# A convolution, a router and eight experts on one core: where the first hidden block lies, and when token rows are gathered

## The chip, the cores and the metric

The kernel runs on one core of a Trainium2 chip. The metric is device time in microseconds (us), the median of timed runs; the profile is of one execution of its own.

## The reference

```python
# first part: a causal convolution along the sequence, softmax weights per head
x_pad = concat([zeros((B, 6, D)), x], axis=1)          # B=8, S=3584, D=192
out = einsum('hk,bskhg->bshg', softmax(weight), windows(x_pad, 7))
# second part, on N = 28672 rows of it
do_compute = x @ w_skip > 0                            # about half of the rows
logits = xc @ w_gate                                   # 8 experts, the best one
gate_w = softmax(logits)[best]
h = maximum(xc @ w1[e], 0)                             # 192 -> 1024
y = gate_w * (h @ w2[e])                               # 1024 -> 192
out[do_compute] = xc + y
```

Rows that the skip score drops keep the convolution's value.

## The kernel before

**Phase 1** goes through the eight batches. For each, TensorE does the convolution, transposes the rows, makes the logits and, by products with one-hot tiles, a list for each expert of the rows that it has to work on. SyncE stores the convolved rows to the output tensor in DRAM (`store_y`, L338). The rows of four batches are in SBUF at a time, in pools that are closed one by one; the pool of batch 5 (`xlast`) becomes `wk3`, and its stores run while batch 7 is routed.

**Phase 2** works in 61 blocks of up to 256 rows of one expert (`us` is 1 or 2 groups of 128). Eight blocks (0 to 7, `NTAIL`) come from a list of the first five batches for experts 0 and 1 and run while the last batches are still routed; six more (8 to 13, one or two groups each) finish these experts from the final lists; the rest are six blocks of each other expert and 11 whose expert is read at run time. For one block:

- `gather` (L737): GpSimd reads the rows into `y` by an indirect DMA, one for each group of 128. There are seven `y` buffers.
- `prep` (L756 to L772): VectorE takes the largest magnitude (`yam`) and a power of two as scale (`ysc`), ScalarE and VectorE split the row into two f16 parts (`yt`), and SyncE transposes them by DMA into `m`. A block of two groups also needs half of a row of `m` copied to the upper partitions by ScalarE (L750).
- `up` (L807, L816): the **first product**, in banks of PSUM `ph`; ScalarE's relu writes the high part `hh` (L820), VectorE the rest `hl` (L822).
- `down` (L850 to L852): the **second product** into `po`, 48 matmuls for two groups. VectorE adds the scaled result to `y` (L832), GpSimd scatters `o` to the output rows (L834).

The program is in the order in which the code is written. In step n of the main loop come `up` of block n+1, with parts of `prep` of later blocks between its banks; the gathers of blocks up to n+5 (`AHEAD`); then `down` of block n, again with parts of `prep`. Before a gather in the first eight steps GpSimd copies one element of `hl` of block n+1 (`after`, `tick`, L732), so that the gather can't start before that part of the first product has been rounded. The table `PSEQ` says how many parts of `prep` of blocks 0 to 2 follow each of the eight heads of the last batch's convolution. The raw weights of an expert are loaded into the buffer `raw` (L206), of which there is one; `wt` holds them split in two f16 parts. Those of expert 2 are loaded from step 6 on. The weights of the first two experts are written back to a scratch tensor (L264).

Of the kernel before, what the change touches and what calls it, by code (L numbers as in the profile page):

```python
# [7 lines left out]
F32 = mybir.dt.float32  # L8
F16 = mybir.dt.float16
# [7 lines left out]
P = 128  # L17
B, S, D = 8, 3584, 192
H, KT = 8, 7
G = D // H  # L20
E, F = 8, 1024
NTOK = B * S
NF = F // P
# [13 lines left out]
BLK = 256  # L37
# [29 lines left out]
E1 = 3  # L67
PIECES = (2,)*5 + (6, 8, 8)

PSEQ = (0,0,0,3,4,4,4,4)  # L70

IL = 4
ROUND = 12582912.0
# [17 lines left out]
def conv_router_moe(ctx: ExitStack, tc: tile.TileContext, x, band, taps, router_weights, weights, out):  # L91
    nc = tc.nc
    const = ctx.enter_context(tc.tile_pool(name="const", bufs=1))
    wst = ctx.enter_context(tc.tile_pool(name="wst", bufs=1))
# [590 lines left out]
    def step7(h):  # L685

        if FIRST[h]:
            if h:
                after(xs[B - 1][0:1, 0, h * G:h * G + 1])
            gather(blocks[int(FIRST[h])])  # L690
        for _ in range(PSEQ[h]):
            prep_piece()
# [3 lines left out]
    def prep_piece():  # L696
        if not preps:
            if begun[0] == PREP0:
                return
            preps.append(prep(blocks[begun[0]]))  # L700
            begun[0] += 1
        if next(preps[0], preps) is preps:
            preps.pop(0)
            prep_piece()
# [26 lines left out]
    def after(t):  # L731
        nc.gpsimd.tensor_copy(tick, t)  # L732

    def gather(k, fixed=True):
        k.y = ybuf[k.n % DEPTH]
        for u in range(k.us):
            rows_apart(nc.gpsimd.indirect_dma_start(  # L737
                out=k.y[:, u, :], out_offset=None, in_=out[0:k.rows, :],
                in_offset=bass.IndirectOffsetOnAxis(ap=k.si[:, u:u + 1], axis=0),
                bounds_check=k.rows - 1, oob_is_err=False), fixed)  # L740

    def paired(k):
        return k.us == 2 and NTAIL <= k.n < NBLK
# [39 lines left out]
    def bank(pools):  # L783
        pools.append(pools.pop(0))
        return pools[-1]

    def up(k, wt):
        k.hh = wk3.tile([P, NF, BLK], F16, tag="hh", bufs=2, name=f"hh{k.n}")
        k.hl = wk3.tile([P, NF, BLK], F16, tag="hl", bufs=2, name=f"hl{k.n}")
        w = k.us * P  # L790
        fs = 2 * BLK // w
        seq = ((OW1, 0), (OW1, 2), (OW1 + F, 1), (OW1L, 0), (OW1L + F, 1))
        phs = {}

        def open_bank(f0):
            phs[f0] = bank(ph_pools).tile([P, 2 * BLK], F32, tag="ph", name=f"ph{k.n}_{f0}").rearrange(
                "p (f w) -> p f w", w=w)

        if paired(k):

            for f0 in range(0, NF, fs):
                open_bank(f0)
            for a in range(0, NF, 2 * fs):
                for j in range(fs):
                    for f, p0, m in ((a + j, 0, 1), (a + fs + j, 64, 3)):
                        o = OW1L + F + f * P
                        nc.tensor.matmul(phs[f - j][:, j, :], wt[p0:p0 + 64, o:o + P], k.m[p0:p0 + 64, m, 0:w],  # L807
                                         start=(j == 0), stop=False, tile_position=(p0, 0), skip_group_check=True)
            seq = seq[:-1]
        for f0 in range(0, NF, fs):  # L810
            if not paired(k):
                open_bank(f0)
            ph = phs[f0]
            for f in range(f0, f0 + fs):
                for n, (o, m) in enumerate(seq):
                    nc.tensor.matmul(ph[:, f - f0, :], wt[:, o + f * P:o + (f + 1) * P], k.m[:, m, 0:w],  # L816
                                     start=(n == 0 and not paired(k)), stop=(n == len(seq) - 1),
                                     skip_group_check=paired(k))
            hh = k.hh[:, f0:f0 + fs, 0:w]
            nc.scalar.activation(hh, ph, AF.Relu)  # L820
            yield
            nc.vector.scalar_tensor_tensor(out=k.hl[:, f0:f0 + fs, 0:w], in0=ph, scalar=0.0, in1=hh,  # L822
                                           op0=ALU.max, op1=ALU.subtract)
# [36 lines left out]
    blocks = []  # L860
# [15 lines left out]
    NTAIL = len(blocks)  # L876
# [6 lines left out]
    NBLK = len(blocks)  # L883
# [40 lines left out]
    wk3 = ctx.enter_context(tc.tile_pool(name="wk3", bufs=2))  # L924
# [147 lines left out]
    gathered, prepped = AHEAD - 1, PREP0  # L1072
# [4 lines left out]
    for n in range(NBLK):  # L1077
        k = blocks[n]
        if listed and len(ph_pools) == 1:
            ph1.close()  # L1080
            wk4 = ctx.enter_context(tc.tile_pool(name="wk4", bufs=1))
            ps_h2 = ctx.enter_context(tc.tile_pool(name="ps_h2", bufs=2, space=PSUM))
            ph_pools.extend((ps_h2, ps_h, ps_h2, ps_h))
            ps_o2 = ctx.enter_context(tc.tile_pool(name="ps_o2", bufs=2, space=PSUM))
            po_pools.extend((ps_o2, ps_o2))
        nxt = 2 if n == NTAIL - 2 else k.e + 1 if k.e is not None and k.e >= NA and n == first_of[k.e] else E
        if nxt < E:
            wts[nxt] = new_wt(nxt)
            bg.append(split_weights(nxt, wts[nxt]))
        if n + 1 < NBLK and n + 1 == first_of.get(blocks[n + 1].e) and (blocks[n + 1].e or 0) >= NA:  # L1090
            background(-1)
        m = n + PREP + 1
        if m < NBLK and blocks[m].l is not None:
            l = blocks[m].l
            dynw[l] = wk4.tile([P, WW], F16, tag="wd", bufs=5, name=f"wd{l}")
            bg.append(dyn_weights(l, dynw[l]))
        far = n + 2
        while far < min(n + PREP + 1 + (n > 4), NBLK) and sum(q.us for q in blocks[n + 2:far]) < 4:
            far += 1
        while prepped < min(far, gathered):  # L1100
            ahead.append(prep(blocks[prepped]))
            prepped += 1
        if n + 1 < NBLK:
            upper_half(n + 1)
            weave(up(blocks[n + 1], weights_of(n + 1)), ahead, PU)
            upper_half(n + 2)
        ready = NBLK if listed and n > 3 else NTAIL
        if n + 1 >= NTAIL - 2:
            while prepped < min(n + 3, gathered):
                ahead.append(prep(blocks[prepped]))  # L1110
                prepped += 1
        while gathered < min(n + AHEAD + 1, ready):
            if n < NTAIL:
                after(blocks[n + 1].hl[0:1, 2 * (gathered % 3):2 * (gathered % 3) + 1, 0])
            gather(blocks[gathered])
            gathered += 1
        if n >= NTAIL - 2:
            next(saves, None)
        weave(down(k, weights_of(n)), ahead, PD)
        if n + 2 < NBLK and not hasattr(blocks[n + 2], "m"):  # L1120
            if prepped < n + 3:
                ahead.append(prep(blocks[prepped]))
                prepped += 1
            finish(ahead.pop(0))
        if n >= NTAIL + 8 and n % 2 == 0 and (n - NTAIL - 8) // 2 < NDYN:
            dyn_lists((n - NTAIL - 8) // 2)
# [4 lines left out]
    with tc.If(left > 0):  # L1131
# [10 lines left out]
        for e in range(E):  # L1142
            first = nc.values_load(lo_hi[0:1, e:e + 1], min_val=0, max_val=NTOK // BLK)
            last = nc.values_load(lo_hi[0:1, E + e:E + e + 1], min_val=0, max_val=NTOK // BLK)
            with tc.For_i(first, last, 1) as i:
                k = Blk()
# [69 lines left out]
```

## Time and profile before

| | us |
|---|---|
| runs | 655.3, 655.6, 663.0 |
| median | 655.6 |
| the profiled execution | 664.3 |
| its span on the core | 662.5 |
| TensorE busy in it | 624.5 |

The profile is of one execution, 8.7 us longer than the median of the runs. Its span leaves out 1.8 us of that execution. A busy time is the union of an engine's instructions, so TensorE was without a matmul for 38 us of the span. In its rows the bracket at the end is the time that the engine stood idle before the instruction and what ended it; "issue" is idle time that nothing in the records ends. PEclk is the granted clock as a share of full speed.

### The profile page before, as it was taken

To read this page: it belongs to the slowest core of one execution; us is meant where nothing else is said; L and a number is where in the kernel's file an instruction comes from. 1 tells how busy PE (TensorE), PEld (TensorE's weight loads), DVE (VectorE), ACT (ScalarE), POOL (GpSimd) and SP (SyncE) were. 2 spreads that over 40 slices of the span, in tenths; PEclk is the share of its full clock that TensorE was granted. 3 is DMA by queue.
4 is the path that set the end of the run, shared out by engine and by line. 5 is a ranking of instruction groups with operands and counts; after the bars stand their busy time and mean duration, and the time that the engine had idled before them with its cause. 6 is when DMAs were issued, how large, how long until landed. Compare 5 with 4: busy or idle time off the path is not lost.

```text
span 662.5 us, 18033 instructions
## 1 busy us (share of the span) xinstructions
PE 624.5 (94%) x6905; PEld 525.8 (79%) x6905; DVE 489.6 (74%) x1380; ACT 340.1 (51%) x665; POOL 266.5 (40%) x298
## 2 busy tenths in 40 slices
PE   7999999988899889999999998999999999999995
PEld 6555565556789778888989887899999988888995
DVE  4296989987797686787887885887878866666642
ACT  3687977876232254445545544544645544444421
POOL 4011111140444445445545545545545554444332
PEclk9999999998999899999999999999999999999998
DMA  8979797673562575773763662663673638999990
GB/s 339 427 328 372 300 400 315 238 236 126 177 197 67 151 186 151 222 196 79 181 188 80 174 187 63 181 178 79 169 191 86 185 79 255 238 337 234 281 241 13
DMA packets 93104, 134.64 MB, mean 203 GB/s; under 512 B 58268, under 2 KB 72670, under 8 KB 90576
## 3 DMA queue, kind: packets, MB, share of 16 engines
q1 hardware_dynamic: 81968, 111.37, 52.9%
q0 software_dynamic: 11040, 22.02, 12.8%
q8 instruction: 56, 0.92, 0.6%
q14 instruction: 40, 0.33, 0.2%
HBM read 72.10 MB, written 50.77 MB: 185 GB/s over the span
## 4 chain that ended last, share of the span: by engine, by line
PE 60%; DVE 1%; issue 1%; ACT 1%; another core or an unknown queue 0%; POOL 0%; POOLq 0%; ACTq 0%
PE ph L816 27%; PE po L852 10%; PE po L850 10%; PE po L851 10%; PE ph L807 4%; ACT hh L820 0%; DVE hl L822 0%; DVE am L214 0%; ACT yt L764 0%; ACT wt L235 0%; ACT m L750 0%; DVE yam L756 0%; DVE o L832 0%; POOL out_dram L834 0%
## 5 line engine op out<-in xcount | busy, mean ns | idle before, releaser
L820 ACT ACTIVATE hh<-ph 128x512 f16<-128x512 f32 x230 | 133.9, 593 | 235.5 <-PE ph L816 159.1
L822 DVE SCALAR_TENSOR_TENSOR hl<-ph,hh 128x512 f16<-128x512 f32 x230 | 157.2, 687 | 100.9 <-ACT hh L820 54.9
L850 PE MATMUL po<-wt,hh 128*128 128x192 f16 x768 | 189.6, 247 | 3.1 <-issue 3.0
L852 PE MATMUL po<-wt,hl 128*128 128x192 f16 x768 | 189.5, 247 | 2.9 <-issue 2.8
L851 PE MATMUL po<-wt,hh 128*128 128x192 f16 x768 | 189.5, 247 | 2.3 <-issue 2.1
L816 PE MATMUL ph<-m,wt 128*128 128x256 f16 (+1 forms) x1680 | 186.9, 269 | 1.7 <-DVE yam L759 1.0
L816 PEld LDWEIGHTS <-wt 128*128 128x128 f16 x1680 | 154.0, 98 | 27.5 <-issue 11.1
L834 POOL DMA_INDIRECT out_dram<-o,rows x82 | 86.4, 1054 | 143.2 <-DVE o L832 113.4
L737 POOL DMA_INDIRECT y<-out_dram,rows x82 | 85.6, 1044 | 25.2 <-issue 22.7
L850 PEld LDWEIGHTS <-hh 128*128 128x128 f16 x920 | 90.2, 98 | 6.0 <-issue 5.2
L852 PEld LDWEIGHTS <-hl 128*128 128x128 f16 x920 | 90.3, 98 | 5.5 <-issue 5.4
L851 PEld LDWEIGHTS <-hh 128*128 128x128 f16 x920 | 90.2, 98 | 4.6 <-issue 4.0
L769 DVE SCALAR_TENSOR_TENSOR yt<-y,ysc,yt 128x64 f16<-128x64 f32 x230 | 58.0, 312 | 3.6 <-ACT yt L764 3.4
L764 ACT ACTIVATE yt<-y,ysc 128x192 f16<-128x192 f32 x115 | 46.2, 447 | 27.7 <-DVE ysc L759 16.3
L832 DVE SCALAR_TENSOR_TENSOR o<-po,yf,y 128x192 f32<-128x192 f32 x115 | 46.4, 414 | 15.3 <-PE po L852 8.9
L313 ACT COPY xy<-pc 128x768 f32<-128x768 f32 x56 | 42.4, 813 | 8.7 <-PE pc L303 6.6
L235 ACT ACTIVATE wt<-raw,ar 128x512 f16<-128x512 f32 x56 | 40.5, 724 | 7.0 <-DVE ar L280 6.7
L303 PE MATMUL pc<-xy,toep 64*64 64x384 f32 x448 | 43.6, 499 | 0.5 <-ACT xy L313 0.5
L254 DVE SCALAR_TENSOR_TENSOR wt<-raw,ar,wt 128x512 f16<-128x512 f32 x56 | 41.7, 745 | 2.7 <-ACT wt L235 2.7
L357 POOL COPY yc<-xy 128x1024 f32<-128x1024 f32 x12 | 12.9, 1074 | 75.4 <-ACT xy L313 31.4
L376 PE MATMUL tp<-ident,xy 128*128 128x128 f32 x256 | 36.4, 285 | 6.9 <-ACT ya L313 4.7
L376 PEld LDWEIGHTS tp<-ident,xy 128*128 128x128 f32 x256 | 27.6, 142 | 18.5 <-ACT ya L313 6.4
(186 smaller groups left out, 814.8 us busy)
## 6 DMA issues: line engine op xcount, KB each, us to landing
xy<-in_x_dram SPq DMA_DIRECT2D x7, 3104.0 KB
wd<-wscr SPq DMA_DIRECT2D x44, 449.0 KB
wscr<-wt SPq DMA_DIRECT2D x84, 128.0 KB
raw<-in_weights_dram SPq DMA_DIRECT2D x16, 512.0 KB
out_dram<-xy SPq DMA_DIRECT2D x5, 1552.0 KB
out_dram<-xy SPq DMA_DIRECT2D x5, 1455.0 KB
raw<-in_weights_dram SPq DMA_DIRECT2D x16, 384.0 KB
out_dram<-xy SPq DMA_DIRECT2D x14, 388.0 KB
```

The lines of the kernel that those rows point to most:

```text
L376: nc.tensor.transpose(tp[:, u, :], src, ident)
L737: rows_apart(nc.gpsimd.indirect_dma_start(out=k.y[:, u, :], out_offset=None, in_=out[0:k.rows, :], in_offset=bass.IndirectOffsetOnAxis(ap= ...
L764: nc.scalar.activation(yt[:, u, 0:D], k.y[:, u, 0:D], AF.Copy, scale=sc[:, u:u + 1])
L769: nc.vector.scalar_tensor_tensor(out=yt[:, u, o:o + b_ - a], in0=k.y[:, u, a:b_], scalar=sc[:, u:u + 1], in1=yt[:, u, a:b_], op0=ALU.mult, ...
L816: nc.tensor.matmul(ph[:, f - f0, :], wt[:, o + f * P:o + (f + 1) * P], k.m[:, m, 0:w], start=(n == 0 and not paired(k)), stop=(n == len(se ...
L820: nc.scalar.activation(hh, ph, AF.Relu)
L822: nc.vector.scalar_tensor_tensor(out=k.hl[:, f0:f0 + fs, 0:w], in0=ph, scalar=0.0, in1=hh, op0=ALU.max, op1=ALU.subtract)
L832: nc.vector.scalar_tensor_tensor(out=o[:, u, 0:D], in0=po, scalar=f2[:, u:u + 1], in1=k.y[:, u, 0:D], op0=ALU.mult, op1=ALU.add)
L834: rows_apart(nc.gpsimd.indirect_dma_start(out=out[0:k.rows, :], out_offset=bass.IndirectOffsetOnAxis(ap=k.si[:, u:u + 1], axis=0), in_=o[: ...
L850: nc.tensor.matmul(pos[u], hh, w2(OW2, f), start=(f == 0), stop=False)
L851: nc.tensor.matmul(pos[u], hh, w2(OW2L, f), start=False, stop=False)
L852: nc.tensor.matmul(pos[u], hl, w2(OW2, f), start=False, stop=(f == NF - 1))
```

## The change

`up` takes the two halves of the relu's result of block 0 from the buffer of the raw weights, which nothing uses at that time, in place of two tiles of `wk3`. `PSEQ` does the parts of `prep` of blocks 0 to 2 earlier in the last batch. The step that gathers now copies an element of `hl` of the next block ahead of each block's gathers to the end, and in steps 4 and 5 it stops at two groups, from step 6 on at four.

```diff
-PSEQ = (0,0,0,3,4,4,4,4)
+PSEQ = (0,0,0,3,6,6,3,3)
...
     def up(k, wt):
-        k.hh = wk3.tile([P, NF, BLK], F16, tag="hh", bufs=2, name=f"hh{k.n}")
-        k.hl = wk3.tile([P, NF, BLK], F16, tag="hl", bufs=2, name=f"hl{k.n}")
+        if k.n == 0:
+            both = wst.tile([P, 2 * F + NF * D], F32, tag="raw", name="h0").bitcast(F16)[:, 0:2 * NF * BLK]
+            k.hh, k.hl = (both[:, o:o + NF * BLK].rearrange("p (f w) -> p f w", w=BLK) for o in (0, NF * BLK))
+        else:
+            k.hh = wk3.tile([P, NF, BLK], F16, tag="hh", bufs=2, name=f"hh{k.n}")
+            k.hl = wk3.tile([P, NF, BLK], F16, tag="hl", bufs=2, name=f"hl{k.n}")
...
+        room = 2 if n < NTAIL - 2 else 4
         while gathered < min(n + AHEAD + 1, ready):
-            if n < NTAIL:
-                after(blocks[n + 1].hl[0:1, 2 * (gathered % 3):2 * (gathered % 3) + 1, 0])
+            if ready == NBLK and blocks[gathered].us > room:
+                break
+            room -= blocks[gathered].us
+            f = 2 * (gathered % 3) if n < NTAIL else 2
+            after(blocks[n + 1].hl[0:1, f:f + 1, 0])
             gather(blocks[gathered])
             gathered += 1
```

TensorE's instructions keep their order; those of the other engines move at these places.

On ScalarE, at the first relu (`ph0_0` is the first bank of block 0; `lg6` and `lt6` are logits of batch 6, `ya7` rows of batch 7 on their way to a transpose). Before:

```order
L389 COPY lt6_1_2252<-pl6_1_2239 128x256 [waits PE_49,Activation_49]
L396 COPY lg6_1972<-pb6_1_2268 128x4x18 [waits PE_49]
L396 COPY lg6_1972<-pb6_1_2268 128x4x18
L764 ACTIVATE yt2_2282<-y2_233,ysc2_2263 128x192 [waits DMASW4_49,DVE_49]
L764 ACTIVATE yt2_2282<-y2_233,ysc2_2263 128x192 [waits DMASW5_49]
L820 ACTIVATE hh0_2311<-ph0_0_2313 128x512 [waits DMAHW5_49,DMAHW3_49,DMAHW6_49,DMAHW0_49,DMAHW7_49,PE_49,Activation_49]
L313 COPY ya7_0_2328<-tp7_0_0_2329 128x512 [waits PE_49]
```

And with the change:

```order
L389 COPY lt6_1_2260<-pl6_1_2247 128x256 [waits PE_49,Activation_49]
L764 ACTIVATE yt2_2267<-y2_233,ysc2_2230 128x192 [waits DMASW4_49,DVE_49]
L764 ACTIVATE yt2_2267<-y2_233,ysc2_2230 128x192 [waits DMASW5_49]
L396 COPY lg6_1972<-pb6_1_2278 128x4x18 [waits PE_49]
L396 COPY lg6_1972<-pb6_1_2278 128x4x18
L824 ACTIVATE h0_2311<-ph0_0_2312 128x512 [waits PE_49,Activation_49]
L313 COPY ya7_0_2327<-tp7_0_0_2328 128x512 [waits PE_49]
```

The relu no longer waits for the DMA queues (the stores of batch 5, whose place `wk3` takes); they are now waited for by the first relu of block 1. The split of block 2 has moved ahead of the logits of batch 6.

On GpSimd, at the end of the first eight blocks (`y1` is block 8's buffer, `y2` block 9's, `y3` block 10's, `y4` block 11's; L834 is the scatter). Before:

```order
L737 DMA y1_230<-out_0_dram,rows_224 128x194
L732 CAST tick_225<-hl5_3226 1x1
L737 DMA y2_233<-out_0_dram,rows_224 128x194 x2
L834 DMA out_0_dram<-o1_2299,rowsa_223 19840x194 x2
L732 CAST tick_225<-hl6_3406 1x1
L737 DMA y3_236<-out_0_dram,rows_224 128x194 x2
L834 DMA out_0_dram<-o2_2301,rowsa_223 19840x194 x2
L732 CAST tick_225<-hl7_3572 1x1
L737 DMA y4_239<-out_0_dram,rows_224 128x194
```

And with the change:

```order
L737 DMA y1_230<-out_0_dram,rows_224 128x194
L838 DMA out_0_dram<-o1_2299,rowsa_223 19840x194 x2
L732 CAST tick_225<-hl6_3398 1x1
L737 DMA y2_233<-out_0_dram,rows_224 128x194 x2
L838 DMA out_0_dram<-o2_2301,rowsa_223 19840x194 x2
L732 CAST tick_225<-hl7_3549 1x1
L737 DMA y3_236<-out_0_dram,rows_224 128x194 x2
L732 CAST tick_225<-hl7_3549 1x1
L737 DMA y4_239<-out_0_dram,rows_224 128x194
```

The gathers of blocks 9 and 10 are each a step later, and from step 8 on each block's gathers stand behind a copy of the next block's `hl`; there are 48 more of these copies in all.

On SyncE's queue, at the same place (`m9` and `m10` are the transposes of blocks 9 and 10, `raw2` loads of the raw weights of expert 2). Before:

```order
L772 DMA_TRANSPOSE m8_3457<-yt8_3441 128x3x128
L772 DMA_TRANSPOSE m9_3525<-yt9_3522 128x3x128 x2
L206 DMA raw2_3595<-in_weights_dram 128x1024 x2
L206 DMA raw2_3595<-in_weights_dram 128x768
L264 DMA wscr_63<-wt0_248 128x1024 x2
L206 DMA raw2_3595<-in_weights_dram 128x768
L772 DMA_TRANSPOSE m10_3671<-yt10_3631 128x3x128 x2
```

And with the change:

```order
L772 DMA_TRANSPOSE m8_3449<-yt8_3433 128x3x128
L206 DMA raw2_3572<-in_weights_dram 128x1024 x2
L206 DMA raw2_3572<-in_weights_dram 128x768
L264 DMA wscr_63<-wt0_248 128x1024 x2
L206 DMA raw2_3572<-in_weights_dram 128x768
L772 DMA_TRANSPOSE m9_3655<-yt9_3608 128x3x128 x2
L264 DMA wscr_63<-wt0_248 128x1024 x2
L772 DMA_TRANSPOSE m10_3802<-yt10_3759 128x3x128 x2
```

Block 9's transposes are now behind the loads of expert 2's raw weights, and block 10's behind two more stores. VectorE and ScalarE do the `prep` of blocks 9 and 10 a step later in the same way, ScalarE that of block 10 just ahead of the copy of block 9's upper half.

## Rows read from the trace of the kernel before

**Rows 1.** Page, part 1: busy us (share of span) x instructions.
```profile
PE 624.5 (94%) x6905; PEld 525.8 (79%) x6905; DVE 489.6 (74%) x1380; ACT 340.1 (51%) x665; POOL 266.5 (40%) x298
```

**Rows 2.** Page, part 4: the chain that ended last, by engine.
```profile
PE 60%; DVE 1%; issue 1%; ACT 1%; another core or an unknown queue 0%; POOL 0%; POOLq 0%; ACTq 0%
```

**Rows 3.** Timeline of PE, first relu: start, us, instruction [idle before <-releaser].
```profile
148.43 1.26 PE L816 MATMUL ph<-m,wt 128*128 128x256 f16 x10
152.39 1.60 PE L376 MATMUL tp<-ident,xy 128*128 128x128 f32 x8 [2.71 <-ACT ya L313]
154.04 2.33 PE L816 MATMUL ph<-m,wt 128*128 128x256 f16 x10
...
158.75 1.04 PE L376 MATMUL tp<-ident,xy 128*128 128x128 f32 x8
```

**Rows 4.** Timeline of ACT, the same place.
```profile
143.43 0.80 ACT L764 ACTIVATE yt<-y,ysc 128x192 f16<-128x192 f32 x2 [1.25 <-DVE ysc L759]
...
151.27 0.60 ACT L820 ACTIVATE hh<-ph 128x512 f16<-128x512 f32 x1 [3.82 <-DMA out_dram<-xy]
```

**Rows 5.** Windows: length, busy us (x) by engine, PEclk, DMA share, GB/s.
```profile
152.40:156.60 4.20, 4.20 (x24) 3.34 (x25) 2.83 (x8) 3.36 (x7) 0.00 (x0) 0.59 0.17 47
```

**Rows 6.** Timeline of DVE, the rest of batch 7's routing.
```profile
151.90 0.69 DVE L822 SCALAR_TENSOR_TENSOR hl<-ph,hh 128x512 f16<-128x512 f32 x1 [1.08 <-ACT hh L820]
...
157.04 0.69 DVE L822 SCALAR_TENSOR_TENSOR hl<-ph,hh 128x512 f16<-128x512 f32 x1 [1.57 <-ACT hh L820]
...
172.76 0.69 DVE L822 SCALAR_TENSOR_TENSOR hl<-ph,hh 128x512 f16<-128x512 f32 x1 [3.58 <-issue]
```

**Rows 7.** Timeline of PE, second product of block 5.
```profile
215.53 0.24 PE L852 MATMUL po<-wt,hl 128*128 128x192 f16 x1 [0.48 <-issue]
216.97 0.24 PE L850 MATMUL po<-wt,hh 128*128 128x192 f16 x1 [1.19 <-issue]
...
218.38 0.32 PE L852 MATMUL po<-wt,hl 128*128 128x192 f16 x1 [1.09 <-issue]
```

**Rows 8.** Timeline of POOL ahead of it and beside it.
```profile
208.27 1.06 POOL L737 DMA_INDIRECT y<-out_dram,rows  x1 [0.96 <-issue]
209.32 0.18 POOL L732 CAST tick<-hl 1x1 f32<-1x1 f16 x1
...
214.96 1.06 POOL L737 DMA_INDIRECT y<-out_dram,rows  x1 [0.16 <-issue]
216.32 1.01 POOL L737 DMA_INDIRECT y<-out_dram,rows  x1 [0.30 <-issue]
```

**Rows 9.** Windows, that second product (columns as in Rows 5).
```profile
213.50:222.26 8.76, 5.92 (x50) 5.13 (x48) 4.59 (x20) 1.96 (x5) 3.25 (x4) 0.81 0.22 58
```

**Rows 10.** Waits of PE: us in total, times, longest us.
```profile
PE po L850 <- issue: 4.0, 7, 1.2
PE po L852 <- issue: 3.3, 5, 1.1
PE po L851 <- issue: 2.3, 6, 0.9
...
PE ph L807 <- ACT m L750: 0.5, 2, 0.3
```

**Rows 11.** Windows, gathers (L737) alone, second products: length, POOL busy (x), PEclk, DMA.
```profile
252.58:258.39 5.81, 2.08 (x2) 1.00 0.65 198
391.89:396.26 4.37, 2.07 (x2) 1.00 0.33 88
...
419.57:424.57 5.00, 2.05 (x2) 1.00 0.79 220
...
501.80:505.86 4.06, 2.09 (x2) 1.00 0.46 108
```

**Rows 12.** Timeline of POOL and of DVE in one clean step.
```profile
333.01 1.05 POOL L737 DMA_INDIRECT y<-out_dram,rows  x1 [0.30 <-issue]
...
333.90 0.69 DVE L822 SCALAR_TENSOR_TENSOR hl<-ph,hh 128x512 f16<-128x512 f32 x1 [0.48 <-issue]
```

## The prediction

> **What bounds the kernel now.** I read the page's busy times first: TensorE is busy for 624.5 of 662.5 us [rows 1], and the chain that ended last is mostly its own [rows 2]. Its instructions keep their order, so the change is worth what it takes from or adds to TensorE's idle and slowed time. I then listed TensorE's waits by what ended them, and read the timelines at the two largest gaps and the windows around them. The reader is to see three things there.
>
> First, at 149.7 to 152.4 TensorE stands still for 2.71 us because ScalarE hasn't copied a PSUM tile [rows 3]. ScalarE stood 3.82 us in front of the first relu, until a store of rows had landed [rows 4]; the copy is the next in its queue. Right after the gap TensorE's granted clock is at its lower level for most of 152.4 to 156.6: 0.59 on average [rows 5], and ten matmuls take 2.33 us where they had taken 1.26 before [rows 3].
>
> Second, in the second product of block 5 TensorE creeps: idle times of 0.48, 1.19 and 1.09 us that end by "issue" [rows 7], while GpSimd has gathers in hand [rows 8]. The clock falls again, to 0.81 on average over 8.76 us [rows 9].
>
> Third, such "issue" waits come back all through phase 2, nearly all in second products: 4.0 + 3.3 + 2.3 = 9.6 us in all [rows 10]. No record says what holds the engine.
>
> **The two executions.** The sum is made against the profiled execution, 664.3 us (span 662.5 and 1.8 around it). The median of the runs is 8.7 us lower. The program is the same, so something that varies is missing in a typical run; the only candidate of that size in the trace is the "issue" waits (9.6) with the clock loss that follows the worst of them (8.76 x 0.19 = 1.7 [rows 9]). I take it that a typical run has (9.6 + 1.7 - 8.7) / 11.3, about a quarter, of them. The wait for the store isn't of this kind: it has its place in the order, and I count it whole in every run.
>
> **The change, part by part.**
>
> *The first relu in `raw`'s place.* The wait for the stores goes: the first relu then needs only its product. TensorE gains the 2.71 us of its gap, and, with no gap, the slow clock: 4.20 x (1 - 0.59) = 1.7 us [rows 5]; together 4.4. The bounds: at least what VectorE can follow. It does the rounding and batch 7's routing in between, and its idle times there that hang on the relu are 1.08 and 1.57 us, 2.65 in all [rows 6]; if VectorE were the bound from there on, no more than that would be gained. At most 4.4 + 1.25, if the wait of ScalarE for block 1's scale [rows 4] came out as well. I take 4.4, since VectorE has another 3.58 us of idle time before 172.8 [rows 6] in which it catches up. The wait itself moves to block 1's relu, the next user of `wk3`, which is four relus on in ScalarE's queue, with the copies of batch 7 between them: nothing. The buffer `raw` is next written for expert 2, after block 0 is done.
>
> *The scales a step earlier.* The scale of block 1 now comes before two list operations on VectorE, so the 1.25 us [rows 4] shrink; block 2's reduction may meet a gather that hasn't landed. Between 0 and 1.25 gained, already the upper bound above; I take 0, as ScalarE is not what TensorE waits for once the store is out of the way.
>
> *At most two groups in steps 4 and 5.* Before, the gathers of blocks 8, 9 and 10 were five, from 208.27 to 217.33, with two scatters between them [rows 8]; now there are one and two in these steps. If the crowd is what held TensorE, its gap (0.48 + 1.19 + 1.09 = 2.8) and the slow clock (1.7) go: 4.4 us of the profiled execution. If it isn't, 0. For a typical run I take a quarter to a third, 1.3.
>
> *Blocks 9 and 10 a step later.* Block 9's transposes now queue on SyncE behind the loads of `raw2`, and on ScalarE the copy of its upper half (L750) stands behind the split of block 10, which in turn needs a later gather. TensorE's nearest waits are those for such a copy elsewhere, 0.5 us for two [rows 10]. The trace has no larger one, so the upper bound is my choice: one short second product (24 of 48 matmuls, some 2 us) for each of the two blocks, 4. I take 0.5.
>
> *48 more copies on GpSimd.* Each takes 0.18 us [rows 8], and GpSimd is 40% busy [rows 1]; they cost nothing themselves. What they do is to hold each block's gathers until the second bank of the next block's first product is rounded. In a clean step the gather started at 333.0 and that rounding at 333.9 to 334.6 [rows 12]: 1.7 us later, so that both gathers of a step begin in the second product. Queued behind them are the scatters of the block before its own, which wait for that second product in any case, and the rows are needed three blocks later. I take 0; the bounds are below.
>
> **The sum**, for a typical run: 655.6 - 4.4 - 1.3 + 0.5 = **650.4**. For an execution like the profiled one it would be 664.3 - 4.4 - 4.4 + 0.5 = 656.0.
>
> **The rivals.**
>
> *The crowd was the cause, in every run.* Then the whole 4.4 of that place comes off the median too: 655.6 - 4.4 - 4.4 = 646.8. For it: the gap lies just where five gathers meet. Against it: the quarter worked out above.
>
> *The gathers have nothing to do with it.* The spacing buys nothing: 655.6 - 4.4 + 0.5 = 651.7. For it: when the gap begins at 215.05 [rows 7], the first of the five is six microseconds old [rows 8], and a second product with both gathers in it can be without any loss [rows 11]. The Trainium skill (DMA: Bandwidth & Descriptors, Queues, rings and completion order) says that a DMA engine takes turns between its queues, a packet from each, so that gathers on GpSimd's queue would not hold up another queue for long; by that rule this rival is the likely one, and the trace, with a DMA share of only 0.22 during the gap [rows 9], doesn't speak against it.
>
> *VectorE is the bound behind the relu.* Only 2.65 of the 4.4 come through, and nothing else: 655.6 - 2.65 = 653.0. For it: those two idle times are all that VectorE has to give before batch 7's lists [rows 6]. Against it: the 3.58 us behind them.
>
> *Blocks 9 and 10 are late.* TensorE waits 2 us for each: 655.6 - 4.4 - 1.3 + 4 = 653.9.
>
> *The new waits put the gathers where they hurt: slower.* In the profiled execution seven second products had both gathers in them. Four kept their 4.06 us (one stands in the rows), the others took 5.81, 4.37 and 5.00 [rows 11]: 3.0 us over, or 0.43 for each of the seven. The change puts both gathers into all of some 46 second products. Of the 9.6 us of such waits [rows 10], 2.8 are those of block 5; with these 3.0 off, some 3.8 are left for about forty other steps, 0.1 each. So this adds 46 x 0.33 = 15 us, and the time would be 655.6 - 4.4 + 15 = 666. It decides from 0.1 us a step on, which eats the 4.4. Against it: the three products that lost time had stores of weights or other DMA work beside them, with the share at up to 0.79, but so did one that lost nothing; and a typical run has less of such waits.
>
> **How the numbers follow.** Forecast (650.4, its own range 648 to 653): 0.36. Crowd in every run (646.8): 0.18. Gathers without part in it (651.7): 0.18. VectorE (653.0): 0.10. Blocks 9 and 10 late (653.9): 0.08. Slower by the new waits (666): 0.10. The range from 645.5 to 656 takes in all but the last, with the bounds of the first term (2.65 to 5.6) around the middle. Two per cent, about what a measurement of this kernel tells from no change, are 13.1 us: none of the cases is faster than 642.5, and 668.7 is reached only by a worse form of the last. So faster 0.04, the same 0.92, slower 0.04.
>
> **What would show it.** Right: no wait of ScalarE for a store at the first relu, no gap of TensorE there, and a granted clock of 1.00 from 150 to 160; block 1's first product some 4 us earlier; in the second product of block 5 no idle time by "issue"; from there to the end second products of 4.06 us. Wrong in the first term: TensorE waiting for VectorE between 160 and 200 by more than now. Wrong in the fourth: TensorE idle in front of L807 of blocks 9 or 10, ended by the copy L750. Wrong in the last: more or longer "issue" waits in second products than now, with gathers at their start.

## The result and the profile after

Timed in turns with the kernel before, 16 runs of each: before 659.64 us in the median (655.3 to 664.87), changed 654.39 (650.69 to 656.37). The medians lie 5.25 us apart. The ratio, which is not that of the medians, is 0.990 with a 95% interval of 0.9877 to 0.9923: 6.6 us faster, 5.1 to 8.1; gains below are by such ratios. The forecast was 650.4 with a range of 645.5 to 656. The forecast's gain of 5.2 is close; its starting point, 655.6, was the median of three runs, and sixteen have 659.64.

The profiled execution of the changed kernel took 652.6 us, its span 650.8. From the first relu on, lines of the changed kernel are four higher than those of before: the first product is L811 and L820, the relu L824, the rounding L826, the second product L854 to L856. Part 1 of its page, for [rows 1]: VectorE, ScalarE and TensorE do the same work, GpSimd has 48 instructions more.

```profile
PE 621.3 (95%) x6905; PEld 525.0 (81%) x6905; DVE 485.9 (75%) x1380; ACT 336.4 (52%) x665; POOL 275.6 (42%) x346
```

The timeline of PE at the first relu, for [rows 3]. No row here or between them has a bracket with an idle time, and the ten matmuls take 1.26 us each time:

```profile
147.81 1.26 PE L820 MATMUL ph<-m,wt 128*128 128x256 f16 x10
...
149.90 1.26 PE L820 MATMUL ph<-m,wt 128*128 128x256 f16 x10
```

ScalarE there, for [rows 4]: the relu waits for its product and no longer for a store. Block 1's split, the first row, waits 0.60 in place of 1.25; block 2's, the second, 0.29, where it had waited for nothing.

```profile
142.34 0.80 ACT L764 ACTIVATE yt<-y,ysc 128x192 f16<-128x192 f32 x2 [0.60 <-DVE yam L756]
...
145.09 0.80 ACT L764 ACTIVATE yt<-y,ysc 128x192 f16<-128x192 f32 x2 [0.29 <-DVE ysc L759]
...
147.07 0.60 ACT L824 ACTIVATE h<-ph 128x512 f16<-128x512 f32 x1 [0.96 <-PE ph L820]
```

The windows (length, busy us by engine, granted clock, DMA share, GB/s) of this place, of block 5's second product, for [rows 5, 9], and of a later stretch:

```profile
150.00:160.00 10.00, 9.92 (x108) 8.11 (x105) 9.64 (x32) 7.86 (x15) 0.17 (x3) 1.00 0.61 212
...
223.30:226.80 3.50, 3.04 (x20) 2.71 (x20) 2.00 (x6) 1.55 (x4) 0.49 (x2) 0.51 0.19 66
208.04:212.00 3.96, 3.96 (x50) 3.96 (x48) 2.85 (x11) 0.60 (x1) 2.45 (x3) 1.00 0.59 112
```

Block 5's second product now takes 3.96 us in place of 8.76, at a clock of 1.00. But the lower clock is there again at 223.3. What stands ahead of it is the same creeping as in [rows 7], now at the end of block 8's first product and the start of block 7's second (timeline of PE):

```profile
220.32 0.44 PE L820 MATMUL ph<-m,wt 128*128 128x128 f16 x5 [0.29 <-issue]
221.05 0.38 PE L820 MATMUL ph<-m,wt 128*128 128x128 f16 x4 [0.29 <-issue]
221.78 0.22 PE L820 MATMUL ph<-m,wt 128*128 128x128 f16 x1 [0.34 <-issue]
222.50 0.24 PE L854 MATMUL po<-wt,hh 128*128 128x192 f16 x1 [0.50 <-issue]
...
223.24 0.25 PE L856 MATMUL po<-wt,hl 128*128 128x192 f16 x1 [0.42 <-issue]
```

These waits and one more at 223.95 are 2.3 us in all; in block 5's second product before the change they were 2.8. GpSimd's timeline shows what meets there, for [rows 8]: block 10's two gathers, which the limit had pushed back, block 11's and two scatters, each some 1.33 us after the one before.

```profile
216.79 1.05 POOL L737 DMA_INDIRECT y<-out_dram,rows  x1 [0.68 <-ACT yt L764]
218.15 1.01 POOL L737 DMA_INDIRECT y<-out_dram,rows  x1 [0.30 <-issue]
...
219.49 1.01 POOL L737 DMA_INDIRECT y<-out_dram,rows  x1 [0.16 <-issue]
220.81 1.02 POOL L838 DMA_INDIRECT out_dram<-o,rowsa  x1 [0.30 <-DVE o L836]
222.14 1.00 POOL L838 DMA_INDIRECT out_dram<-o,rowsa  x1 [0.31 <-issue]
```

The waits of PE (us in total, times, longest), for [rows 10]. Issue waits of second products fell from 9.6 to 2.6; the wait for the copy L750 rose from 0.5 to 3.5:

```profile
PE ph L811 <- ACT m L750: 3.5, 4, 2.5
...
PE po L854 <- issue: 1.2, 3, 0.5
...
PE po L855 <- issue: 0.7, 2, 0.5
PE po L856 <- issue: 0.7, 2, 0.4
```

The longest is at block 13, at 259.20. Timelines of PE (block 12's first product and that wait) and of ScalarE there:

```profile
250.89 3.67 PE L820 MATMUL ph<-m,wt 128*128 128x256 f16 x32
...
259.20 0.59 PE L811 MATMUL ph<-m,wt 64*128 64x256 f16 x7 [2.45 <-ACT m L750]
```

```profile
254.17 1.08 ACT L824 ACTIVATE hh<-ph 128x512 f16<-128x512 f32 x2 [4.24 <-PE ph L820]
...
257.05 1.06 ACT L824 ACTIVATE hh<-ph 128x512 f16<-128x512 f32 x2
258.00 0.72 ACT L235 ACTIVATE wt<-raw,ar 128x512 f16<-128x512 f32 x1
258.74 0.40 ACT L750 COPY m<-m 64x256 f16<-64x256 f16 x1
```

The copy stands in ScalarE's order behind block 12's relus and a part of the splitting of expert 2's weights. In an experiment with the gathers of before (e2) it came at 258.46, and TensorE, 2 us later there than here, waited 0.23. It isn't only that TensorE is earlier: the first of these relus needs 8 of block 12's 32 matmuls, which end at 251.94, and begins at 254.17, 2.2 us behind them and behind four indirect DMAs that follow each other from 248.34 on. In e2 it begins 0.1 us behind them. The loss comes with the waits in front of the gathers: e3, which has them alone, loses 2.57 us at block 13, e4 with the limit alone 0.50.

### The profile page after: what moved, and what is told of

Its sections match the earlier page's. It is cut to its first block, busy times and chain, and to the rows that moved or that the text cites. A ratio compares the mean times of both kernels' runs of the same rounds, so it can differ in the third digit from the quotient of the medians.

```text
span 650.8 us, 18171 instructions
## 1 busy us (share of the span) xinstructions
PE 621.3 (95%) x6905; PEld 525.0 (81%) x6905; DVE 485.9 (75%) x1380; ACT 336.4 (52%) x665; POOL 275.6 (42%) x346
## 5 line engine op out<-in xcount | busy, mean ns | idle before, releaser
L824 ACT ACTIVATE hh<-ph 128x512 f16<-128x512 f32 x226 | 127.3, 589 | 220.2 <-PE ph L820 176.0
L820 PE MATMUL ph<-m,wt 128*128 128x256 f16 (+1 forms) x1680 | 186.3, 268 | 2.5 <-DVE yam L759 1.0
L854 PE MATMUL po<-wt,hh 128*128 128x192 f16 x752 | 185.7, 247 | 1.2 <-issue 1.2
L855 PE MATMUL po<-wt,hh 128*128 128x192 f16 x752 | 185.7, 247 | 0.7 <-issue 0.7
L856 PE MATMUL po<-wt,hl 128*128 128x192 f16 x752 | 185.7, 247 | 0.7 <-issue 0.7
L826 DVE SCALAR_TENSOR_TENSOR hl<-ph,hh 128x512 f16<-128x512 f32 x226 | 153.0, 685 | 37.0 <-ACT hh L824 28.1
L820 PEld LDWEIGHTS <-wt 128*128 128x128 f16 x1680 | 153.6, 98 | 27.9 <-issue 11.7
L737 POOL DMA_INDIRECT y<-out_dram,rows x82 | 86.0, 1048 | 38.5 <-ACT hh L824 21.5
L854 PEld LDWEIGHTS <-hh 128*128 128x128 f16 x904 | 88.8, 98 | 2.8 <-issue 2.2
L855 PEld LDWEIGHTS <-hh 128*128 128x128 f16 x904 | 88.7, 98 | 2.7 <-issue 2.1
L856 PEld LDWEIGHTS <-hl 128*128 128x128 f16 x904 | 88.8, 98 | 0.0
L732 POOL CAST tick<-hl 1x1 f32<-1x1 f16 x57 | 11.0, 194 | 80.5 <-DVE hl L826 68.7
L214 DVE TENSOR_REDUCE am<-raw 128x1 f32<-128x512 f32 x56 | 37.5, 676 | 5.6 <-DMA raw<-in_weights_dram 5.5
```

The costliest lines, as they stand in the source:

```text
L737: rows_apart(nc.gpsimd.indirect_dma_start(out=k.y[:, u, :], out_offset=None, in_=out[0:k.rows, :], in_offset=bass.IndirectOffsetOnAxis(ap= ...
L854: nc.tensor.matmul(pos[u], hh, w2(OW2, f), start=(f == 0), stop=False)
L855: nc.tensor.matmul(pos[u], hh, w2(OW2L, f), start=False, stop=False)
L856: nc.tensor.matmul(pos[u], hl, w2(OW2, f), start=False, stop=(f == NF - 1))
```

## The experiments

The runs e1 to e4, e5 to e8 and e9 to e12 were on three different chips, called A, B and C; the kernel before took up to 17 us longer on one than on another. The chip of the first comparison isn't on record; its traces have issue waits, as those on A and C do. For each trace, three stretches: the start of block 5's second product, from there to the start of block 16's first product, and from there to the end of the span (us, from the timelines of PE).

| kernel | chip | median; before's | ratio (95%) | to block 5 | to block 16 | to the end |
|---|---|---|---|---|---|---|
| before | | 659.64 | | 213.50 | 75.90 | 373.13 |
| changed | | 654.39; 659.64 | 0.990 (0.9877 to 0.9923) | 208.04 | 75.56 | 367.18 |
| e1 relu only | A | 655.54; 658.24 | 0.996 (0.9929 to 0.9992) | 208.21 | 75.72 | 367.19 |
| e2 relu, scales | A | 655.47; 658.24 | 0.9939 (0.9902 to 0.9977) | 208.45 | 74.76 | 369.25 |
| e3 waits only | A | 659.26; 658.24 | 1.0005 (0.9971 to 1.004) | 212.27 | 77.53 | 366.76 |
| e4 limit only | A | 657.3; 658.24 | 0.9993 (0.9958 to 1.0028) | 213.86 | 73.95 | 372.21 |
| e5 change, copy early | B | 643.54; 645.72 | 0.9969 (0.9954 to 0.9983) | 206.14 | 68.97 | 364.77 |
| e6 e5, limit to the end | B | 664.74; 645.72 | 1.0293 (1.0253 to 1.0332) | 206.22 | 76.48 | 381.51 |
| e7 e2 less gathers | B | 639.96, one run | | 206.34 | 67.63 | 364.08 |
| e8 e2 less scatters | B | 642.81, one run | | 206.19 | 70.38 | 364.30 |
| e9 before | C | 664.88, one run; 662.96 | | 211.87 | 76.62 | 374.51 |
| e10 as e2 | C | 658.95; 662.96 | 0.994 (0.991 to 0.9971) | 208.07 | 76.68 | 376.14 |
| e11 changed | C | 657.05; 662.96 | 0.9915 (0.9884 to 0.9945) | 208.28 | 79.07 | 368.63 |
| e12 e2, late waits | C | 656.09; 662.96 | 0.9901 (0.9872 to 0.993) | 208.47 | 76.44 | 371.53 |

**e1.** The kernel before, with the first part of the change:

```diff
+        if k.n == 0:
+            both = wst.tile([P, 2 * F + NF * D], F32, tag="raw", name="h0")...
```

> The kernel before with one part of the change: block 0's relu result in the raw weights' place. The prediction's first term: 4.4 us faster (the gap of 2.71 at the first relu and the slow clock of 1.7 behind it gone; granted clock 1.00 from 150 to 160), with ScalarE's wait of 1.25 for block 1's scale still there. Rival, VectorE is the bound behind the relu: 2.65 faster, with TensorE waiting more between 160 and 200. Rival, the store wait belongs to the profiled execution alone: 0.

2.6 us faster by the ratio (0.5 to 4.7), an interval that holds 4.4 and 2.65 alike. The traces tell them apart: the first column falls from 213.50, 212.27, 213.86 and 211.87 in the four traces without this part to 208.04 to 208.47 in the six with it (chip B's left out), 4.6 in the mean. VectorE isn't the bound.

**e2.** And with the second part:

```diff
-PSEQ = (0,0,0,3,4,4,4,4)
+PSEQ = (0,0,0,3,6,6,3,3)
```

> The kernel before with two parts of the change: the relu result in the raw weights' place and the scales of blocks 0 to 2 earlier; gathers as before. The prediction (scales worth 0): as e1, 4.4 faster. Rival read from the changed kernel's trace, in which the work at 192 us came 5.65 earlier: the 1.25 of ScalarE's wait for the scale comes out as well, 5.65 faster, 1.2 better than e1. Rival, these two parts are all that the change gives: 6.6 faster, as the whole change.

Against e1 on the same chip 0.8 us faster, plus or minus 2.1, and block 5 starts at 208.45 against 208.21. The scales are worth nothing that can be seen; the 5.65 of the one pair of traces was the first relu's alone, in an execution that had the slow clock.

**e3.** The waits from step 8 on, alone:

```diff
-            if n < NTAIL:
-                after(blocks[n + 1].hl[0:1, 2 * (gathered % 3):2 * (gathered % 3) + 1, 0])
+            f = 2 * (gathered % 3) if n < NTAIL else 2
+            after(blocks[n + 1].hl[0:1, f:f + 1, 0])
```

> The kernel before with one part of the change: from step 8 on each block's gathers wait for the second bank of the next block's first product; no limit of two groups, relu and scales as before. The prediction: 0. Rival read from the two traces (issue waits of TensorE fell from 9.6 to 2.6 us, most of them in steps that only this part touches): up to 9.6 - 2.8 = 6.8 faster in an execution like the profiled one, and a quarter to a half of it, 1.7 to 3.4, in the median. Rival on the other side, as the prediction had it: 15 slower.

No difference in the runs: between 1.9 faster and 2.6 slower. In the trace the last stretch is the shortest on that chip, 366.76 (e1, without these waits, has 367.19), and no second product of it has an issue wait, but the middle one is longer: TensorE waits 2.57 us for the copy of block 13 and the slow clock follows.

```profile
264.06 1.01 PE L807 MATMUL ph<-m,wt 64*128 64x256 f16 x7 [2.57 <-ACT m L750]
265.00 4.70 PE L816 MATMUL ph<-m,wt 128*128 128x256 f16 x32
```

The 32 matmuls behind it took 4.70 us; at the full clock they take 3.67.

**e4.** The limit alone (`room`, without the waits from step 8 on).

> The kernel before with one part of the change: at most two groups gathered in steps 4 and 5; no waits from step 8 on. The prediction: 1.3 faster in the median, 4.4 where the issue waits of block 5's second product and the slow clock behind them go in every run. Rival read from the changed kernel's trace, where the same creeping shows three blocks later: the stall only moves, 0, with issue waits and a low clock in the second product of block 7 or in block 8 instead. Rival, blocks 9 and 10 late: 2 to 4 slower, with TensorE waiting in front of their first products for the copy of the upper half.

0.5 faster, between 2.8 faster and 1.8 slower; by time the smaller gain can't be told from none. The trace decides the mechanism: block 5's second product is whole again, and 2.1 us of issue waits stand in block 8's first product and block 7's second, with a slow clock behind, where the changed kernel has them. The stall moves.

**e5.** The changed kernel, with block 13's copy ahead of block 12's relus:

```diff
             upper_half(n + 1)
+            if n == 11:
+                upper_half(n + 2)
             weave(up(blocks[n + 1], weights_of(n + 1)), ahead, PU)
```

> The changed kernel with one more edit: ScalarE's copy of block 13's upper half (L750) stands ahead of block 12's relus in place of behind them. In the changed kernel's trace TensorE waits 2.45 us for it at 259 us, and its transposes had been issued 15 us before. Theory, the work gained ahead is given back there because the copy stands behind VectorE's and ScalarE's splitting of weights and behind block 12's relus: that wait is gone and the time is 1.5 to 2.5 lower than the changed kernel's, some 8 to 9 under the kernel before. Rival, the banks of block 12's product come free no earlier than the copy came: TensorE waits for hl (L826) in its place, 0 to 0.5 lower.

The wait at block 13 is gone. What that is worth isn't shown, since the changed kernel didn't run on this chip. And chip B is another case: the kernel before took 645.72 there, and e5 is only 2.0 us faster (1.1 to 3.0). The list of PE's waits has none that ends by "issue", although GpSimd's five indirect DMAs follow each other as in the changed kernel:

```profile
214.64 1.05 POOL L737 DMA_INDIRECT y<-out_dram,rows  x1 [0.68 <-ACT yt L764]
216.00 1.01 POOL L737 DMA_INDIRECT y<-out_dram,rows  x1 [0.30 <-issue]
...
218.68 1.02 POOL L838 DMA_INDIRECT out_dram<-o,rowsa  x1 [0.30 <-DVE dk L1008]
220.01 1.00 POOL L838 DMA_INDIRECT out_dram<-o,rowsa  x1 [0.31 <-issue]
```

With no stall ahead of it, TensorE comes to block 9 before block 9's rows are there (timeline of PE):

```profile
222.04 0.27 PE L811 MATMUL ph<-m,wt 64*128 64x256 f16 x1 [1.37 <-DMA m<-yt]
223.79 0.59 PE L811 MATMUL ph<-m,wt 64*128 64x256 f16 x7 [1.49 <-ACT m L750]
```

That is the price of the limit, 2.9 us; in the changed kernel's own trace it was 0.20, since the stall at 220 had given the rows time.

**e6.** As e5, with the limit of two groups in all steps:

```diff
-        room = 2 if n < NTAIL - 2 else 4
+        room = 2
```

> As e5, and the limit of two groups a step holds in all steps, so that gathers of blocks 10 and 11 no longer follow each other and two scatters (five indirect DMAs in a row from 216.8 us on in the changed kernel, with 3.65 us of issue waits and a slow clock behind them). Theory, the crowd makes the stall: the issue waits at 218 to 224 fall under 1.5, no slow clock there, 3 to 5 lower than e5. Rival, the stall moves a step further once more: the same issue waits within 20 us behind, 0. Rival on the other side, the gathers stay a step late from there on and the scales wait for them: TensorE waits for L750 or m, 1 to 5 higher than e5.

The rival on the other side, and four times its size: 18.9 us slower than the kernel before. Each gather stays a step late to the end, and TensorE waits for the copy again and again; the granted clock was 0.984 over the run, against 0.997 in e5. The waits of PE:

```profile
PE ph L811 <- ACT m L750: 11.3, 10, 2.5
```

**e7 and e8.** The kernel of e2 without four gathers, and without two scatters:

```diff
+        if k.n in (9, 10):
+            return
```

```diff
+            if k.n == 4:
+                return
             rows_apart(nc.gpsimd.indirect_dma_start(
                 out=out[0:k.rows, :], ...
```

> The kernel of e2 without the gathers of blocks 9 and 10 (left out: these two blocks work on rows that were in their buffers before). In e2 the second product of block 5 has 3.1 us of issue waits, from 2.6 us after the first of two scatters to 1.8 after the last of two gathers. Theory, TensorE's short matmuls are held while indirect DMAs of either kind are under way: half of it is left, 1 to 1.8 us, at its beginning, and no slow clock behind it. Rival, the gathers alone do it: under 0.3. Rival, neither does (transposes, stores or something that no record shows): 3 as before.

> The kernel of e2 without the two scatters of block 4 (left out: that block's rows keep the convolution's value), the gathers as in e2. Theory, indirect DMAs of either kind hold TensorE: the issue waits in block 5's second product begin only some 2.6 us after the first gather and come to 0.5 to 1.5. Rival, gathers alone: 3 as in e2. Rival, scatters alone: under 0.3. Rival, neither: 3.

PE's waits in both have none that ends by "issue", but so it is in e5 and e6 on that chip, which have all gathers and scatters. They tell nothing of the cause. (The waits that the expectations of e6 and e7 put at 3.65 and 3.1 us are 2.3 and 2.4 in the traces.)

**e9.** The kernel before, for its trace on the chip of e10 to e12.

> The kernel before itself, for its trace beside the next three on the same chip: the kernel before took 658.2 us in the median beside e1 to e4 and 645.7 beside e5 to e8, and none of the last four had an issue wait of 0.28 us or more in a second product. Theory, the issue waits and the slow clock behind them are the chip's or its surroundings', and the kernel's order only decides what they hit: where the median is near 645, this trace has under 1 us of issue waits in second products, the whole gap of 2.71 at the first relu, and a span near 645; where it is near 658, 5 to 10 us of them.

The chip (C) is one of the slower kind, and the trace has 8.5 us of issue waits in second products:

```profile
PE po L852 <- issue: 3.6, 7, 1.0
PE po L851 <- issue: 3.0, 7, 0.8
...
PE po L850 <- issue: 1.9, 3, 1.1
```

It also shows when they come. Two of them, on PE and on GpSimd; the first row of each pair on PE is the second product's start, then the matmul at which it stops, then the next:

```profile
333.66 0.25 PE L850 MATMUL po<-wt,hh 128*128 128x192 f16 x1
...
334.98 0.25 PE L851 MATMUL po<-wt,hh 128*128 128x192 f16 x1
335.50 0.24 PE L852 MATMUL po<-wt,hl 128*128 128x192 f16 x1 [0.27 <-issue]
...
420.03 0.25 PE L850 MATMUL po<-wt,hh 128*128 128x192 f16 x1
...
423.00 0.25 PE L850 MATMUL po<-wt,hh 128*128 128x192 f16 x1
423.60 0.24 PE L851 MATMUL po<-wt,hh 128*128 128x192 f16 x1 [0.35 <-issue]
```

```profile
332.17 1.05 POOL L737 DMA_INDIRECT y<-out_dram,rows  x1 [0.31 <-ACT hh L820]
...
417.41 1.28 POOL L834 DMA_INDIRECT out_dram<-o,rows  x1 [6.34 <-DVE o L832]
418.99 1.00 POOL L834 DMA_INDIRECT out_dram<-o,rows  x1 [0.31 <-DVE yam L759]
420.30 1.05 POOL L737 DMA_INDIRECT y<-out_dram,rows  x1 [0.30 <-issue]
421.65 1.01 POOL L737 DMA_INDIRECT y<-out_dram,rows  x1 [0.30 <-issue]
```

The stop comes 1.3 us into the one product and 3.0 into the other, but 2.8 and 2.7 us after the first gather of the step. So it is with all 14 such stops behind 290 us in this trace, where two matmuls start 0.3 us or more apart (a fifteenth, at 408.8, is long and has scatters just ahead): 2.3 to 2.9 us after the gather, 1.2 to 3.9 into the product.

The first gather isn't alone, though. The last four rows are one string: two scatters and two gathers, each started less than 1.8 us after the one before, and the stop comes 1.35 us after the last of them. In the six traces without late waits on the gathers (before, e1, e2, e4, e9, e10) there are 215 such strings of four between 290 and 605 us. Second products stop in 57 steps there, each time behind the third or fourth of a string; most strings have no stop behind them. The waits of the change break the strings up. GpSimd in e11, where the two scatters ahead had started at 411.87 and 413.45, and the windows of that second product and of the first product behind it, both without loss:

```profile
415.69 0.18 POOL L732 CAST tick<-hl 1x1 f32<-1x1 f16 x1 [1.25 <-DVE hl L826]
416.55 1.21 POOL L737 DMA_INDIRECT y<-out_dram,rows  x1 [0.68 <-ACT yt L764]
```

```profile
414.49:418.54 4.05, 4.05 (x51) 3.89 (x49) 3.50 (x10) 4.00 (x9) 1.86 (x3) 1.00 0.67 203
418.54:422.60 4.06, 4.06 (x42) 3.47 (x42) 4.03 (x11) 1.96 (x5) 2.74 (x3) 1.00 0.75 216
```

Where the gather starts within the products doesn't decide it. In the four traces with waits (changed, e3, e11, e12) the time 2.3 to 2.9 us after the first gather still lies in the second product in 63 steps, and one of them has a stop; in the six without, 54 of 220 have. That it is the string is read from the traces; no experiment breaks the strings up in another way.

**e10.** As e2, on chip C.

> The kernel of e2 again (relu in the raw weights' place and the earlier scales, gathers as before), beside the whole change. Theory: 4.4 to 5.65 faster than the kernel before on any chip; where there are no issue waits it is faster than the whole change by the 2 to 3 us that blocks 9 and 10 wait there for their rows (1.37 for the transposes and 1.49 for the copy L750 in e5). Rival: the whole change is faster here too, by 2 or more.

4.0 us faster than before (1.9 to 6.0), an interval that holds the expectation; here the rival is right that the whole change is faster, by 2.3 us, plus or minus 2.2, which is barely clear of none.

**e11.** The changed kernel on chip C.

> The changed kernel again. Where there are no issue waits: 0 to 2.5 faster than the kernel before (4.4 to 5.65 from the relu and the scales, less 3 for block 9 and up to 2 for block 13), with TensorE waiting in front of L811 of blocks 9 and 13. Where there are: 5 to 8 faster, as in the first comparison. Rival: the same ratio as there, 0.99, on any chip.

5.6 us faster (3.6 to 7.7): inside the expectation for a chip with issue waits, and no ratio that holds on any chip, since e5, which has the whole change, gained 2.0 on B. Its block 13 waits longer, with the slow clock behind (timeline of PE):

```profile
260.24 1.01 PE L811 MATMUL ph<-m,wt 64*128 64x256 f16 x7 [3.08 <-ACT m L750]
261.19 6.07 PE L820 MATMUL ph<-m,wt 128*128 128x256 f16 x32
```

**e12.** The relu, the scales, and the waits from step 14 on only:

```diff
-            if n < NTAIL:
-                after(blocks[n + 1].hl[0:1, 2 * (gathered % 3):2 * (gathered % 3) + 1, 0])
+            if n < NTAIL or n >= 14:
+                f = 2 * (gathered % 3) if n < NTAIL else 2
+                after(blocks[n + 1].hl[0:1, f:f + 1, 0])
```

> The relu and the scales as in the change, the gathers of the first 14 steps as before, and the waits of the gathers for the next first product only from step 14 on. Theory: it keeps the gain of e10 and takes no part in what the limit of two groups costs; where there are no issue waits it is as e10, within 0.5, and 2 to 3 faster than e11; where there are, 2 to 3 faster than e10 and within 1 of e11. Rival, the waits in the later steps cost something themselves: 1 or more slower than e10 where there are no issue waits.

6.6 us faster than before (4.6 to 8.5) and 2.9, plus or minus 2.1, faster than e10: the waits do it, without the limit. Against the changed kernel it is 0.7 better, plus or minus 1.8, so no more than equal. Its trace has a few stops left; the one at 354.27 comes 2.8 us after the first of two scatters (351.48), with no gather in the 4 us before it. There too it is a string of four: two gathers at 348.75 and 350.15, then the scatters. So the gathers needn't come last in it.

## Why the prediction was right, and where not

The gain of 5.2 was near the 6.6 measured (5.1 to 8.1), but as a sum of terms two of which were wrong in opposite directions: in part that is luck. By stretches, means over the traces of chips with issue waits: 4.6 gained up to block 5, 1.3 lost between blocks 5 and 16 (77.3 in the changed kernel and e11, against 76.0 in the six traces without limit or early waits), 4.5 gained behind (367.5 in the three traces with waits from step 8 on, 372.1 in the six without any, which spread from 367.2 to 376.1; with e12, whose waits cover nearly all of this stretch, 368.5 and a gain of 3.5).

- **The first relu, 4.4: right**, 4.6. All of the store wait came out with the first part alone. Its make-up was other than I wrote: without the slow clock (e3, e9) the stretch shrinks by 3.8, more than the gap of 2.71, and the slow clock, which I counted whole in every run, was there in two of four traces of kernels with the gap.
- **The scales, 0: right** (e2 against e1).
- **At most two groups, 1.3 gained: failed.** I took it that spacing the gathers dissolves the crowd. It moves it three blocks on, where it costs 2.3 us of issue waits in place of 2.8, and a slow clock again.
- **Blocks 9 and 10 late, 0.5: mis-sized and partly elsewhere.** Where no stall gives them time, block 9 costs 2.9 (e5), inside my bound of 4; where one does, 0.2 to 0.3. Block 10 even gains: without the limit TensorE waits 0.55 to 2.56 us in its first product (2.45 for the copy L750 in e9, the kernel before on chip C), with it 0.16 to 0.84. I took the nearest row of one trace in which the copy was never late, and it is late in another trace of the same kernel. By single traces the limit alone (e4) makes the middle stretch 2.1 shorter than the 76.0, the waits alone (e3) 1.5 longer.
- **48 copies, 0: failed, and the rival that had them cost 15 too.** They are worth 3.5 to 4.5 us in the last stretch in the traces of chips with issue waits, and cost 2.45 to 3.08 at block 13, which I hadn't looked at. I counted in which product a gather starts. What goes with the stops is how many indirect DMAs stand in one string ahead of them, and the waits break up the strings of two scatters and two gathers. The timed runs support it less sharply: e12 against e10 shows 2.9, e3 alone shows none; its loss at block 13 eats part of the gain, and why its median shows nothing of the rest isn't settled.
- **The typical run: failed.** From three runs I concluded that a quarter of the issue waits is present. Sixteen runs put the median 4.0 us higher, which is all of the distance between forecast and result (654.4 - 650.4).
- **The rivals.** "The gathers have nothing to do with it" is refuted by e12 against e10, which differ in the waits on the gathers alone, on a chip with issue waits. The rule of the Trainium skill that I set beside it (DMA: Bandwidth & Descriptors, Queues, rings and completion order: a DMA engine takes turns between its queues) is not refuted: the first matmuls that stop wait for no transfer that the trace shows. It says nothing of what TensorE does while one lands. "VectorE is the bound" is refuted by the 4.6.

What holds TensorE stays open. The instruction fetch isn't it as far as the trace shows: during the 3.93 us of the stall at 212.86 in e9, the DMA queues moved gathers, a scatter and transposes, and no packet of a queue of instructions; the next such packet comes at 220.22, after TensorE has worked on for 3.4 us without a stop (queue, kind: packets, MB, share):

```profile
q0 software_dynamic: 126, 0.28, 29.5%
q1 hardware_dynamic: 416, 0.10, 12.4%
```

Nor is it the crowd by itself, since chip B has the crowd and not the stall: e5 to e8 have 84 strings of four or five between 290 and 605 us, and no stop. And what is held isn't the second product alone. Where ScalarE stands idle over 0.3 us ahead of a relu, its start tells when a bank of the first product was there for it: on B at most 0.38 us after the recorded end of the bank's last matmul. In the six traces without the waits 43 to 56 relus start over 0.6 us after it, up to 5.9, in the four with waits 13 to 22, though TensorE's own rows show hardly a gap there. Whether the stall in block 5's second product needs the gathers, the scatters or both could not be shown by e7 and e8, which ran on B.

## What to carry to other kernels

Look at what else stands in the same string of transfers, and not only at the product in which a transfer starts. When a crowd is spread, ask what dense stretch the next crowd falls on. And before an edit that lets the leading engine arrive earlier, go through the other engines' orders for the first thing that will now be late: here a copy whose rows had landed 8 us before, behind work that nobody waited for.

## What the runs showed of the hardware

- The same program took 645.7 us on one chip and 658.2 and 663.0 on two others. PE's waits in e5 to e8 have none that ends by "issue"; every trace on A and C has some. The whole change gained 5.6 us on C (3.6 to 7.7); with one edit more it gained 2.0 on B (1.1 to 3.0).
- On A and C second products (192 columns) stop behind the third or fourth of a string of indirect DMAs, in e9 for 0.3 to 0.9 us from one matmul's start to the next; 57 steps in six traces have such a stop, with 215 strings of four. Where five follow each other, TensorE gets on only about every 0.7 us for 4 us (220.32, 221.05, 221.78, 222.50 and 223.24 above), and the granted clock falls to its lower level (1.2 of 2.4 GHz; 0.51 on average from 223.3 to 226.8) behind it.
- A wait of 2.57 or 3.08 us of TensorE was followed by the lower clock (32 matmuls in 4.70 and 6.07 in place of 3.67), one of 2.45 in the changed kernel was not; nor were the waits of 2.81 and 2.94 at the first relu in e3 and e9 (granted clock 1.00), where those of 2.71 and 3.23 in the kernel before and e4 were (0.59 and 0.68). The length of the wait alone doesn't decide it.
